# The second product of blocks 4 and 5 by Strassen's scheme, and prepared weights stored whole

## The chip, the cores and the metric

One core of a Trainium2 chip runs the whole program. The metric is device microseconds from start to end of one execution, as the median of several. On the core, PE (TensorE) multiplies matrices, DVE (VectorE) and ACT (ScalarE) do elementwise work, POOL (GpSimd) does a little at the start, and SP (SyncE) only issues DMAs. Each engine works its instructions in the order in which the program lists them.

## The reference

A windowed attention over 4 x 768 tokens gives x of 3072 x 512. Two dense layers follow, each with two products and a bend between them:

```
x   = attention(q, k, v, mem_k, mem_v)        # 3072 x 512
h   = x @ w_in1;   g = h * clip(h + 3, 0, 6) / 6;   x2  = g @ w_out1     # 512 x 2048, 2048 x 512
h2  = x2 @ w_in2;  g2 = max(0.01 * h2, h2);         out = g2 @ w_out2
```

All inputs but the weights are fp32; the weights come as 64-bit floats and are decoded on the chip.

## The kernel before, in words

**Tiling.** The 3072 tokens are six blocks of 512 columns (N), numbered 0 to 5. The 2048 hidden features are 16 tiles (f) of 128 rows, the 512 model features four tiles of 128. Every product is of fp32 values in two parts: a value is rounded to fp32r by a cast on ACT (high part), and DVE subtracts that from the value (low part). A product of two such values is three matmuls: high x high, low x high, high x low. So a plain tile of a product, 128 hidden rows against 512 model features and 512 tokens, is 4 x 3 = 12 matmuls of 128 x 128 by 512 columns (`hidden`, line 856, and `output`, line 903).

**Layer one, blocks 0 to 3,** is plain: `hidden` and `output` alternate, while the attention of later tokens runs between them. Blocks 0 and 1 run their first eight hidden tiles (partly in two half-width pieces for block 1), store a half sum of the output in DRAM (`half`), and add it when the other eight tiles are done.

**Pairs.** Blocks 4 and 5 are pair -1 of layer one; blocks 0-1, 2-3 and 4-5 are pairs 0, 1 and 2 of layer two. A pair's two blocks and the weights are cut into a 2 x 2 scheme, and a product of 2 x 2 quarters is made with seven quarter products instead of eight (Winograd's form of Strassen's scheme, numbers 1, 6, 5, 7 and then 2, 3, 4). `seven` (line 1136) makes the first product of a pair: for each of eight tiles i, seven products of 2 x 3 = 6 matmuls (line 1156), added up by DVE from four PSUM banks, then bent by ACT. Its banks are the set h, h, hx, hx for even i and the set of four y for odd i, but for pair -1 always h, h, hx, hx. `second` (line 1245) makes the second product of pairs 0 to 2: seven numbers n, and for each of them eight tiles i of 6 matmuls (line 1300); for each, ACT and DVE cut the right operand into high and low (lines 1288, 1289). `x_pair` (line 959) loads the right operands of a pair's first product from DRAM, forms the sums and cuts them: eight loads, 22 DVE and 14 ACT operations a pair. The second product of blocks 4 and 5 is plain: `output` for block 4 stands between the tiles of pair -1's first product, and block 5's bent values go to DRAM (`later`) and come back (`back_b`) for 16 tiles of `output` after it.

**Prepared weights.** `prepare` (line 1041) makes the seven left operands of tile i of weight 1i, 2i or 2o (first digit the layer; i the first product, o the second). For 2i and 2o it decodes two tiles (`decode`, line 354: one ACT and four DVE operations each, two of them with two tensor operands, into two `wm` buffers); for 1i it adds high and low again (`joined`). Then four sums of 256 columns are formed in place by DVE (line 1065) and all seven operands are cut into high and low parts of 256 columns (ACT line 305, DVE line 308) in `ys` buffers and stored to DRAM (`keep`, line 1032), 256 KB each. One preparation begins when the two `wm` buffers of the one before are done (`chain`). `left` (line 1087) loads two operands, both parts, 512 KB, into a `w` buffer when a product needs them; six such loads form a ring. There are 33 `w` buffers of 4 KB a partition for everything.

**What sets the order.** The program's text is written out by a planner (`schedule`, line 94). Each piece of work (`add`) has an engine, a duration, a key and the work it follows. A key counts PE work: 12 matmuls are 3 units. A piece is offered when its key is at most 60 units (`AHEAD`) ahead of progress; of the pieces offered the engine with the least key is taken first, where preparations count 60 units more (`late=LATE`). They also don't begin near the end of a plain output's sum (`ends`). The preparations' keys are the list `PLAN` plus `B0` = 24. Layer one's plain blocks are 68 items (pairs of `hidden` and `output`) of 6 units, so pair -1 begins at 408. `seq2` (line 328) is the order of PE's work from there on, and gives `pos_p` and `pos_q`, the positions of the products of `seven` and `second`. In `left` a load's key is 22 units before its product.

## Time and profile before

| | us |
|---|---|
| median of 3 runs | 1069.92 (1068.75 to 1071.33) |
| the profiled execution | 1069.66 |
| its span, first to last instruction | 1067.6 |
| PE busy | 1045.2 (7536 matmuls) |
| DVE busy | 777.5 |
| ACT busy | 569.0 |

The profile is of one execution. Busy shares are means over stages of different kinds: the start with attention, layer one up to 441 us, pair -1 with the plain outputs of blocks 4 and 5 up to 606.9 us, then six stages of 76.2 us: the first and the second product of pairs 0, 1 and 2. The chain of work that ended last tells what the end waited for; windows tell how full each engine is in each stage; timelines show when one instruction follows another. Recorded matmuls overlap, so their mean duration is not the time that one adds.

### The profile page before, as it was taken

The numbers are of one execution on the slowest core, as the hardware profiler recorded it, in microseconds if no ns is written. First come the engines' busy times: TensorE is split into PE (matmuls) and PEld (weight loads), VectorE is DVE, ScalarE is ACT, GpSimd is POOL, SyncE is SP. The second block draws the span as 40 slices with busy tenths as digits, with TensorE's granted clock in tenths as the row PEclk, the third lists the DMA queues.
The fourth block names the chain that finished last, engine by engine and source line by source line (L and its number), as shares of the span: only waits on it lengthen the run. The fifth ranks groups of instructions, "written<-read, shape, count | busy, mean of one in ns | idle before, by whom it ended". The sixth has DMA issues, their size and how long they took to land.

```text
span 1067.6 us, 20633 instructions
## 1 busy us (share of the span) xinstructions
PE 1045.2 (98%) x7536; PEld 864.4 (81%) x7536; DVE 777.5 (73%) x1469; ACT 569.0 (53%) x1416; POOL 14.5 (1%) x27
## 2 busy tenths in 40 slices
PE   5899999999999999999999999999999999999998
PEld 4778988888888888888888888888888888888886
DVE  4997993757776569898897688898465794465663
ACT  5678674656666666555456354565243553243432
POOL 2100000000000000000000000000000000000000
PEclk9899999999999999999999999999999999999999
DMA  9899234556776857899999599968656697666763
GB/s 208 221 245 279 104 112 132 184 164 191 222 223 198 260 180 251 285 313 323 321 332 355 199 344 358 341 213 321 229 208 233 243 321 248 217 232 227 269 214 119
DMA packets 124469, 257.22 MB, mean 241 GB/s; under 512 B 12752, under 2 KB 47056, under 8 KB 124368
## 3 DMA queue, kind: packets, MB, share of 16 engines
q1 hardware_dynamic: 124368, 255.90, 72.5%
q8 instruction: 60, 0.98, 0.4%
q14 instruction: 41, 0.34, 0.1%
HBM read 184.55 MB, written 71.30 MB: 240 GB/s over the span
## 4 chain that ended last, share of the span: by engine, by line
PE 91%; DMA 3%; DVE 2%; ACT 1%; SPq 1%; issue 1%; DVEq 0%; ACTq 0%
PE y L903 19%; PE h L856 15%; PE y L1300 12%; PE y L1156 11%; PE hx L1156 10%; PE h L1156 8%; PE h L1300 6%; PE hx L1300 3%; DMA w<-in_raw 2%; PE hx L903 2%; PE h L903 2%; PE at L533 2%; PE at L472 1%; PE at L522 1%; DMA w<-in_w1o 1%
## 5 line engine op out<-in xcount | busy, mean ns | idle before, releaser
L903 PE MATMUL y<-g,w 128*128 128x512 f32 (+1 forms) x1008 | 236.2, 382 | 0.1
L903 PEld LDWEIGHTS y<-g,w 128*128 128x128 f32 x1008 | 181.7, 188 | 36.1 <-ACT ys L933 0.3
L308 DVE TENSOR_TENSOR w<-w 128x512 fp32r<-128x512 f32 (+1 forms) x208 | 137.0, 688 | 17.6 <-ACT w L305 16.5
L856 PE MATMUL h<-xh,w 128*128 128x512 f32 (+1 forms) x544 | 131.6, 383 | 3.6 <-DVE xl L308 2.1
L856 PEld LDWEIGHTS h<-xh,w 128*128 128x128 f32 x544 | 98.4, 190 | 23.9 <-ACT xh L305 2.2
L1300 PE MATMUL y<-w 128*128 128x512 f32 x384 | 90.0, 389 | 0.0
L1131 ACT ACTIVATE w<-w 128x512 f32<-128x512 f32 x48 | 30.3, 632 | 107.8 <-DVE w L1214 79.2
L1300 PEld LDWEIGHTS y<-w 128*128 128x128 f32 x384 | 72.1, 188 | 15.0
L308 DVE TENSOR_TENSOR ys<-wm,ys 128x256 fp32r<-128x256 f32 x168 | 68.3, 426 | 19.3 <-ACT ys L305 18.5
L305 ACT CAST ys<-wm 128x256 fp32r<-128x256 f32 x168 | 62.7, 405 | 34.9 <-DVE wm L377 16.8
L1156 PE MATMUL hx<-w 128*128 128x512 f32 x336 | 80.7, 389 | 0.0
L868 ACT ACTIVATE r<-h,three 128x512 f32<-128x512 f32 (+1 forms) x68 | 45.4, 668 | 56.0 <-PE h L856 55.7
L1156 PEld LDWEIGHTS hx<-w 128*128 128x128 f32 x336 | 63.1, 188 | 13.1
L305 ACT CAST w<-w 128x512 fp32r<-128x512 f32 x116 | 66.8, 618 | 10.6 <-DVE w L308 3.8
L871 DVE SCALAR_TENSOR_TENSOR r<-r,h 128x512 f32<-128x512 f32 (+1 forms) x68 | 44.3, 652 | 36.5 <-ACT r L868 36.1
L856 PE MATMUL h<-xl,w 128*128 128x512 f32 (+1 forms) x272 | 70.8, 382 | 0.0
L305 ACT CAST g<-r 128x512 fp32r<-128x512 f32 (+1 forms) x86 | 52.0, 604 | 34.5 <-DVE r L871 21.5
L308 DVE TENSOR_TENSOR g<-r,g 128x512 fp32r<-128x512 f32 (+1 forms) x86 | 56.9, 662 | 15.8 <-ACT g L305 15.4
L305 ACT CAST g<-w 128x512 fp32r<-128x512 f32 x50 | 31.0, 623 | 59.3 <-PE y L1300 31.2
L856 PEld LDWEIGHTS h<-xl,w 128*128 128x128 f32 x272 | 49.5, 190 | 9.5
L308 DVE TENSOR_TENSOR g<-w,g 128x512 fp32r<-128x512 f32 x50 | 33.9, 689 | 26.9 <-ACT g L305 26.7
L1156 PE MATMUL y<-w 128*128 128x512 f32 x216 | 50.9, 389 | 0.0
(216 smaller groups left out, 1758.2 us busy)
## 6 DMA issues: line engine op xcount, KB each, us to landing
w<-kept2i SPq DMA_DIRECT2D x84, 512.0 KB
w<-kept2o SPq DMA_DIRECT2D x84, 512.0 KB
kept1i<-ys SPq DMA_DIRECT2D x56, 256.0 KB
kept2i<-ys SPq DMA_DIRECT2D x56, 256.0 KB
kept2o<-ys SPq DMA_DIRECT2D x56, 256.0 KB
w<-kept1i SPq DMA_DIRECT2D x28, 512.0 KB
w<-later SPq DMA_DIRECT2D x20, 512.0 KB
a<-in_raw SPq DMA_DIRECT2D x40, 224.0 KB
```

The lines of the kernel that those rows point to most:

```text
L305: nc.scalar.copy(out, in_) if e == "ACT" else engine(e).tensor_copy(out=out, in_=in_)
L308: engine(e).tensor_tensor(out=out, in0=a, in1=b, op=ALU.subtract)
L472: nc.tensor.matmul(ps.t[h * CHUNK:(h + 1) * CHUNK, par, i * W:(i + 1) * W], qk[h // 2].t[r, gp, (h % 2) * G + c * CHUNK:(h % 2) * G + (c + ...
L522: nc.tensor.transpose(pt.t[:, i // NC, (i % NC) * 128:(i % NC + 1) * 128], e.t[:, i].rearrange("p r k -> p (r k)"), ident)
L533: nc.tensor.matmul(pv.t[(h % 2) * D:(h % 2 + 1) * D, par, (h // 2) * 2 * G + i * CHUNK:(h // 2) * 2 * G + (i + 1) * CHUNK], v[h // 2].t[r, ...
L856: nc.tensor.matmul(h.t[:, :n], w.t[:, 1 if p == 1 else 0, k * 128:(k + 1) * 128], x[:, k, c0:c0 + n], start=(p == 0 and k == 0), stop=(p = ...
L868: nc.scalar.activation(out=make(r)[:, :n], in_=h.t[:, :n], func=AF.Relu, bias=three[:, 0:1], scale=1.0)
L871: nc.vector.scalar_tensor_tensor(out=r.t[:, :n], in0=r.t[:, :n], scalar=6.0, in1=h.t[:, :n], op0=ALU.min, op1=ALU.mult)
L903: nc.tensor.matmul(bank(banks[d])[:, c0:c0 + n], w.t[:, 1 if p == 1 else 0, d * 128:(d + 1) * 128], g.t[:, 1 if p == 2 else 0, :n], start= ...
L1131: return add(lambda e: nc.scalar.activation(out=at(), in_=at(), func=AF.Prelu, alpha=0.01), {"ACT": act(N)}, key, after=[after], uses=uses)
L1156: nc.tensor.matmul(bank(to), t.t[:, o, l, kt * 128:(kt + 1) * 128].bitcast(F32R), operand(p, name, 1 if q == 2 else 0, kt).bitcast(F32R), ...
L1300: nc.tensor.matmul(bank(to[d]), w.t[:, o, 1 if q == 1 else 0, d * 128:(d + 1) * 128].bitcast(F32R), g.t[:, 1 if q == 2 else 0], start=(fre ...
```

## The change

The second product of pair -1 is made by `second` too: the plain `output` calls of blocks 4 and 5, `back_b` and the extra `later` space are gone, and `seven` bends pair -1's sums with layer one's gate (`gated`, `bent`: a Relu on ACT and one operation on DVE, the second half of the buffer of sums as scratch) and keeps them as it does for the other pairs. `second`'s ends scale by 1/6 for pair -1 and store to `spill`. This needs prepared 1o weights: eight more calls of `prepare`.

1o, 2i and 2o are stored whole (`whole`): no cutting into high and low, the four sums are formed in two `ys` buffers, and each of the seven operands is stored as 128 KB. `left` loads four operands, 512 KB, into a `w` buffer, at most about seven half-loads ahead, and cuts two of them at a time into another `w` buffer with an ACT cast and a DVE subtraction of 512 columns (keys 12 units before the product, at most four such pieces ahead). The product's second part waits for the low half. 1i stays as it was, with a ring of five.

`PLAN` is new: 1i and 1o alternate, two per 18 units from key 140 on, then the eight 2i and the eight 2o, one per 18 units from 274 on. 1o preparations, and every second one of the first six of 2i and 2o, use the two `st` buffers and a chain of their own (`chains`). All of them wait until the last plain weights are cut. Layer one runs block 1's second eight tiles ahead of block 0's, and block 1 keeps its sum in PSUM without the way over DRAM. `x_pair` of pairs 0 to 2 has keys 24 and 16 units ahead of the stage. All pairs use alternating sets of banks.

The diff, cut to its core (the lines left out put the 1/6, the gate and `spill` into `seven` and `second`, and pass both waits on the parts of a left operand):

```diff
@@ -44,11 +44,14 @@
 LEFT_OF = {1: "a11", 2: "a12", 3: "s4", 4: "a22", 5: "s1", 6: "s2", 7: "s3"}
 ORDER = FIRST + THEN
 RING, OPS = 6, 6
+RING_LESS = 28
+BOTH = 6
+SPLIT = ("1i",)
+LEAD, RING_V, SPLITS = 28, 7, 4
 LATE, BEFORE = 60, 7
 JOINED = 8
-PLAN = [(172 + 16.5 * (k + k // 2), "1i", k) for k in range(8)]
-PLAN += [(172 + 16.5 * (3 * k + 2), ("2i", "2o")[k % 2], k // 2) for k in range(4)]
-PLAN += [(172 + 16.5 * (12 + k), ("2i", "2o")[k % 2], 2 + k // 2) for k in range(12)]
+PLAN = [(140 + 18 * (k // 2), ("1i", "1o")[k % 2], k // 2) for k in range(16)]
+PLAN += [(274 + 18 * k, ("2i", "2o")[k // 8], k % 8) for k in range(16)]
...
-    items += [("1", j, f, 0, N) for j in range(TWICE) for f in range(KF // 2, KF)]
+    items += [("1", j, f, 0, N) for j in (1, 0) for f in range(KF // 2, KF)]
...
-    for i in range(KF // 2 + 1):
-        if i < KF // 2:
-            seq2 += [("p", -1, i, n) for n in FIRST]
-            if i == 0:
+    for p in range(-1, PAIRED):
+        for i in range(KF // 2):
+            seq2 += [("p", p, i, n) for n in FIRST]
+            if p < 0 and i == 0:
                 seq2.append(("y", PLAIN - 1, KF - 1))
-            seq2 += [("p", -1, i, n) for n in THEN]
-        if i:
-            seq2 += [("y", PLAIN, 2 * i - 2), ("y", PLAIN, 2 * i - 1)]
-    seq2 += [("y", PLAIN + 1, f) for f in range(KF)]
-    for p in range(PAIRED):
-        for i in range(KF // 2):
-            seq2 += [("p", p, i, n) for n in FIRST + THEN]
+            seq2 += [("p", p, i, n) for n in THEN]
...
-        halves = (KF // 2, KF) if j < TWICE else (KF,)
+        halves = (KF // 2, KF) if j == 0 else (KF,)
         begin = c0 == 0 and f in (0, *halves)
         end = f + 1 in halves
         if begin:
-            ybuf[lay, j] = banks_of(j > PLAIN)
+            ybuf[lay, j] = banks_of(False)
...
+        k = add(lambda e: nc.vector.tensor_tensor(out=make(m, ([128, 512], F32)), in0=w.t[:, 0].bitcast(F32), in1=w.t[:, 1].bitcast(F32), op=ALU.add), {"DVE": dve(512)}, key, after=[*wtask[which, f], *splits[-2:], *gate], allocs=[m], uses=[w], late=LATE)
...
+    def whole(which, i, raws, l, key):
+        at = {"a11": (0, 0), "a12": (0, 256), "a21": (1, 0), "a22": (1, 256)}
+        if which[1] == "o":
+            at["a12"], at["a21"] = at["a21"], at["a12"]
+        sums = [Buf("ys"), Buf("ys")]
+        at |= {"s1": (2, 0), "s3": (2, 256), "s2": (3, 0), "s4": (3, 256)}
+        homes, made_by = [*raws, *sums], {}
+        def part(name):
+            c, o = at[name]
+            return made(homes[c])[:, o:o + 256]
+        def form(name, x, y, op):
+            new = homes[at[name][0]]
+            made_by[name] = add(lambda e: nc.vector.tensor_tensor(out=part(name), in0=part(x), in1=part(y), op=op), {"DVE": dve(256)}, key, after=[*l, *(made_by[n] for n in (x, y, "s1") if n in made_by)], allocs=[new] if at[name][1] == 0 else [], uses=[b for b in homes if b.users and (b is not new or at[name][1])], late=LATE)
+        def keep_whole(name):
+            q = [LEFT_OF[m] for m in ORDER].index(name)
+            slot = 7 * i + q if which[1] == "i" else KF // 2 * q + i
+            kdone[which, slot] = add(lambda e: nc.sync.dma_start(out=kept[which][slot // 4, :, slot % 4], in_=part(name)), {"SP": dma(131072, 300.0)}, key + 2, after=[made_by[name]] if name in made_by else l, uses=[homes[at[name][0]]], late=LATE)
+        for name in ("a11", "a12", "a22"):
+            keep_whole(name)
+        for name, x, y, op in (("s1", "a21", "a22", ALU.add), ("s2", "s1", "a11", ALU.subtract), ("s3", "a11", "a21", ALU.subtract), ("s4", "a12", "s2", ALU.subtract)):
+            form(name, x, y, op)
+            keep_whole(name)
...
-            line, place = (chain, "wm") if i < JOINED else (alone, "st")
+            line, place = (chain, "wm") if which != "1o" else (alone, "st")
             parts = [joined(which, 2 * i + c, key, place, line) for c in range(2)]
         else:
-            line, parts = chain, []
+            turn_of = len(decoded) // 2 % 2 and len(decoded) < 2 * BOTH
+            line, parts = chains[turn_of], []
             for c in range(2):
-                parts.append(decode(src, 2 * i + c, key + 6 * c, after=splits[-2:] + decoded[-2:-1], gate=chain, late=LATE))
+                parts.append(decode(src, 2 * i + c, key + 6 * c, after=splits[-2:] + decoded[-2:-1], gate=line, place=("wm", "st")[turn_of], late=LATE))
...
+        if which not in SPLIT:
+            whole(which, i, raws, l, key)
+            return
...
-        m = 7 * KF // 2 * (p + 1) + (7 * KF // 4 if which == "o" and p >= 0 else 0) + slot // 2
-        if p < 0:
-            m += 7 * KF // 4
+        m = 7 * KF // 2 * (p + 1) + (7 * KF // 4 if which == "o" else 0) + slot // 2
         which = ("1" if p < 0 else "2") + which
+        if m not in ring and which not in SPLIT:
+            group = slot // 4
+            if (p, which, group) not in loaded:
+                r = Buf("w")
+
+                def fn(e):
+                    nc.sync.dma_start(out=make(r, ([128, 4, 256], F32)), in_=kept[which][group])
+
+                k = add(fn, {"SP": dma(524288, 360.0)}, key - LEAD, after=[*(kdone[which, s] for s in range(4 * group, 4 * group + 4)), *rlast.get(m - RING_V, [])], allocs=[r])
+                loaded[p, which, group] = r, k
+            r, k = loaded[p, which, group]
+            t, o = Buf("w"), 2 * (slot // 2 % 2)
+            hi = add(lambda e: copy(e, make(t, ([128, 2, 2, 256], F32R))[:, :, 0], r.t[:, o:o + 2]), {"ACT": act(512)}, key - 12, after=[k, *rlast.get(m - SPLITS, [])], allocs=[t], uses=[r])
+            lo = add(lambda e: minus(e, t.t[:, :, 1], r.t[:, o:o + 2], t.t[:, :, 0].bitcast(F32)), {"DVE": dve(512)}, key - 11.5, after=[hi], uses=[r, t])
+            ring[m] = t, (hi, lo)
...
-            k = add(fn, {"SP": dma(524288, 360.0)}, key - 22, after=[kdone[which, slot], kdone[which, slot + 1], *rlast.get(m - RING + (p < 0), [])] + (xtask[-1, "b11" if slot < 4 else "t4"][slot >= 4][:1] if p < 0 else []), allocs=[t])
-            ring[m] = t, k
+            k = add(fn, {"SP": dma(524288, 360.0)}, key - 22, after=[kdone[which, slot], kdone[which, slot + 1], *rlast.get(m - RING + (m < RING_LESS), [])] + (xtask[-1, "b11" if slot < 4 else "t4"][slot >= 4][:1] if which == "1i" else []), allocs=[t])
+            ring[m] = t, (k, k)
...
-        product(part(0), N, [wl, *xhi, *need], allocs=alloc, uses=[u for u in us if u not in alloc], count=2)
-        product(part(1), N, [], uses=us, count=2)
+        product(part(0), N, [wl[0], *xhi, *need], allocs=alloc, uses=[u for u in us if u not in alloc], count=2)
+        product(part(1), N, [wl[1]], uses=us, count=2)
...
+        def bent(at, k, uses):
+
+            if p >= 0:
+                return leak(at, key, k, uses)
+            done["spare"] = [gated(at, at, [k, *done.get("spare", [])], u(1), [ut, *uses])]
+            return done["spare"][0]
...
+            k = product(part(order[:2]), N, [wl[0], hi, *need], allocs=to if fresh else (), uses=us + ([] if fresh else to), count=2)
+            product(part(order[2:4]), N, [wl[1]], uses=us + to, count=2)
...
-                x_pair(j + 1, pos_p[j + 1, 0, 1] - 58, 20)
+                x_pair(j + 1, pos_p[j + 1, 0, 1] - 24, 8)
             second(j, f, n[0])
         else:
-            if j > PLAIN:
-                if f == 0:
-                    x_pair(0, pos_p[0, 0, 1] - 40, 18)
-                back_b(f)
             output("1", j, f, 0, N)
```

## Rows read from the trace of the kernel before

**Rows 1.** The page: span and instructions; PE's busy tenths in 40 slices.
```profile
span 1067.6 us, 20633 instructions
...
PE   5899999999999999999999999999999999999998
```

**Rows 2.** Chain of work that ended last: start us, length us, what.
```profile
441.00 2.72 PE h L1156 x12
...
552.52 10.88 PE y L903 x48
606.92 2.72 PE h L1156 x12
...
683.08 10.88 PE h L1300 x48
...
759.24 2.72 PE h L1156 x12
...
1042.12 21.77 PE y L1300 x96
```

**Rows 3.** Windows by stage: us, busy (count) of PE PEld DVE ACT POOL, clock, DMA, GB/s.
```profile
36.40:120.00 83.60, 80.39 (x959) 68.14 (x960) 73.52 (x161) 62.44 (x189) 1.47 (x1) 0.97 0.80 228
120.00:441.00 321.00, 321.00 (x3239) 264.26 (x3238) 227.84 (x461) 197.77 (x607) 2.91 (x3) 1.00 0.61 191
441.00:606.90 165.90, 165.90 (x734) 137.37 (x733) 140.23 (x277) 85.60 (x166) 0.00 (x0) 1.00 0.88 309
606.90:683.10 76.20, 76.20 (x338) 63.10 (x337) 59.01 (x114) 36.75 (x74) 0.00 (x0) 1.00 0.97 341
683.10:759.20 76.10, 76.10 (x337) 63.00 (x337) 63.98 (x106) 40.72 (x72) 0.00 (x0) 1.00 0.75 272
759.20:835.40 76.20, 76.20 (x338) 63.10 (x337) 44.01 (x67) 27.55 (x45) 0.00 (x0) 1.00 0.66 233
835.40:911.60 76.20, 76.20 (x338) 63.10 (x337) 57.99 (x94) 38.37 (x70) 0.00 (x0) 1.00 0.76 264
987.70:1063.90 76.20, 76.18 (x337) 62.74 (x335) 45.35 (x72) 30.61 (x56) 0.00 (x0) 1.00 0.60 204
```

**Rows 4.** Timelines of DVE and ACT, layer two: start us, length us, engine, what.
```profile
730.81 5.50 DVE L308 TENSOR_TENSOR w<-w 128x512 f32<-128x512 f32 x9
...
700.86 0.62 ACT L305 CAST g<-st 128x512 fp32r<-128x512 f32 x1 [1.29 <-PE hx L1300]
701.38 0.62 ACT L305 CAST xh<-w 128x512 fp32r<-128x512 f32 x1
...
640.88 0.42 DVE L1065 TENSOR_TENSOR wm<-wm 128x256 f32<-128x256 f32 x1
641.21 0.69 DVE L1214 TENSOR_TENSOR w<-y,w 128x512 f32<-128x512 f32 x1
```

**Rows 5.** What DVE waited for, 441 to 606.9 us: us in total, times, longest.
```profile
DVE w L308 <- PE hx L903: 2.9, 2, 2.7
DVE xh L308 <- ACT xh L305: 2.9, 2, 2.2
```

**Rows 6.** Windows of 20 us (columns as in rows 3).
```profile
540.00:560.00 20.00, 20.00 (x90) 16.57 (x89) 19.40 (x38) 11.37 (x22) 0.00 (x0) 1.00 0.89 320
700.00:720.00 20.00, 20.00 (x90) 16.57 (x89) 20.00 (x35) 12.63 (x23) 0.00 (x0) 1.00 0.62 214
```

**Rows 7.** Single lines: decodes after 441 us, stores of prepared weights, and SP's waits.
```profile
L373 DVE SCALAR_TENSOR_TENSOR wm<-w,wm x22: 681/686/694, 442.6 to 657.6; 128x512 uint32<-128x512 uint32 x22
...
L1032 SPq DMA_DIRECT2D kept2o<-ys x56: 319/320/543, 299.2 to 673.3; - x56
...
SPq L1098 <- PE y L1300: 20.1, 15, 3.7
```

**Rows 8.** DMA issues of the page: operation, count, KB each.
```profile
w<-kept2i SPq DMA_DIRECT2D x84, 512.0 KB
w<-kept2o SPq DMA_DIRECT2D x84, 512.0 KB
kept1i<-ys SPq DMA_DIRECT2D x56, 256.0 KB
kept2i<-ys SPq DMA_DIRECT2D x56, 256.0 KB
kept2o<-ys SPq DMA_DIRECT2D x56, 256.0 KB
```

More of the change, by code (lines that the diff above doesn't have):

```diff
@@ L1028, in tile_attn_moe_moe2 @@
     chain, kdone, decoded, alone = [], {}, [], []
+    chains = (chain, alone)
     def keep(which, slot, src, after, uses, key):
@@ L1037, in joined @@
         w, m = wbuf[which, f], Buf(place)
-        k = add(lambda e: nc.vector.tensor_tensor(out=make(m, ([128, 512], F32)), in0=w.t[:, 0].bitcast(F32), in1=w.t[:, 1].bitcast(F32), op=ALU.add), {"DVE": dve(512)}, key, after=[*wtask[which, f], *gate], allocs=[m], uses=[w], late=LATE)
+        k = add(lambda e: nc.vector.tensor_tensor(out=make(m, ([128, 512], F32)), in0=w.t[:, 0].bitcast(F32), in1=w.t[:, 1].bitcast(F32), op=ALU.add), {"DVE": dve(512)}, key, after=[*wtask[which, f], *splits[-2:], *gate], allocs=[m], uses=[w], late=LATE)
@@ L1170, in put @@
         def put(r, after):
-            held["b", p, i] = add(lambda e: nc.sync.dma_start(out=later[p, i], in_=r.t), {"SP": dma(N * 512, 330.0)}, key, after=[after], uses=[r])
+            held["b", p, i] = add(lambda e: nc.sync.dma_start(out=later[p % (PAIRED + 1), i], in_=r.t), {"SP": dma(N * 512, 330.0)}, key, after=[after], uses=[r])
         def u(c):
@@ L1349, in second @@
                 before = [qdone[p, 5, d]] if n == 7 else [qdone[p, 6, d]]
-                q = plus(lambda s=s: s.t, from_, at(with_), key, [k, *before], allocs=[s], uses=[with_, bk])
+                q = sum_of(lambda s=s: made(s), at(with_), [k, *before], allocs=[s], uses=[with_, bk])
                 qdone[p, n, d] = q
```

102 lines of the change are left out of this document (40 added, 62 removed).

## The prediction

> **What bounds the kernel now.** I read three views, in this order. The page first: PE, the matrix engine, is busy in every slice of the span from the third on [rows 1]. A busy share alone proves little, since matmuls overlap in the record, so I read the chain of work that ended last for their spacing. It is nothing but PE work from 441 us to the end: 12 matmuls take 2.72 us, 48 take 10.88 us, 96 take 21.77 us [rows 2], so one costs 0.2267 us wherever it stands. A first-product stage of a layer-two pair is 8 x 7 x 6 = 336 matmuls = 76.2 us, and so is a second-product stage: the stages begin at 606.92, 683.08 and 759.24 us [rows 2]. Then the windows by stage: from 120 us on PE is busy for all of each window, at a granted clock of 1.00 [rows 3]. Nothing that DVE, ACT or the DMAs do after 120 us is waited for. The time is a count of matmuls, until another engine fills up. In these stages DVE is the nearest: 64.0 of 76.1 us in the second stage of pair 0, against 40.7 for ACT [rows 3].
>
> **Matmuls.** The plain second product of blocks 4 and 5 goes: 2 blocks x 16 tiles x 12 = 384. In its place come 8 tiles x 7 products x 6 = 336. The difference, 48 x 0.2267 = 10.88 us, lies wholly on the path.
> The Trainium skill, "TensorE: Matmul & The Clock Gate", section "Wait — 56ns, not 53.3ns?", gives 215.7 ns from start to start for 512 columns at full clock; the rows show 226.7 ns. By the page the 48 would be worth 10.4 us, as an estimate; the row is this kernel's own.
>
> **Splitting the left operands at each use.** The weights of 2i, 2o and 1o now come whole, so each stage that uses them gets 28 ACT casts and 28 DVE subtractions of 512 columns. Nine such DVE operations in a row take 5.50 us with 0.69 for one alone, so their pitch is (5.50 - 0.69)/8 = 0.60 us; ACT's casts start 0.52 us apart [rows 4]. That is 28 x 0.60 = 16.9 us of DVE and 28 x 0.52 = 14.6 us of ACT per stage. What it lies beside: the first stage of pair 1 has 67 DVE operations, its second stage 94 (22 of them from `x_pair`), the second stage of pair 2 has 72 [rows 3]. With 28 more, at 0.60 us: 57, 73.4 and 60 us of 76.2. It fits, by a thin 3 us where `x_pair` falls into the stage. ACT goes from 38.4 to 53 us in the same stage: covered. If DVE's cover is gone, each lacking operation costs PE 0.60 us.
>
> **Preparing the weights.** A 2i or 2o preparation loses seven halvings into high and low: 19 DVE operations become 12. Two-operand ones of 512 columns cost 0.60 us, those of 256 columns 0.33 [rows 4]; I take 0.33 for the two one-operand steps of a decode as well. So 4 x 0.60 + 8 x 0.33 = 5.1 us instead of 7.4. The eight new 1o preparations cost 2 x 0.60 + 4 x 0.33 = 2.5 us each, 20 us in all, before 441 us. Between 120 and 441 us DVE is busy 227.8 of 321.0 us [rows 3], so 93 us are free for them.
>
> **The stretch where DVE gets tight.** Today the first product of blocks 4 and 5 is mixed with the plain products, and 441 to 606.9 us has 140.2 us of DVE work in 165.9 [rows 3]. After the change three stages stand there: the first product of pair -1 (348 matmuls with the last tile of block 3, 78.9 us), its second product (76.2 us), and the first product of pair 0, up to some 7 us before its end, when the last 2o weights must be in DRAM to be read back and split (69 us). Together 224 us. DVE work in them without preparations, at 0.60 us: 102 operations (11 for each of 8 tiles, less 2 that fall later, and 16 run ahead for the second product) = 61.4 us; 122 (as counted for pair 1) = 73.4 us; about 75 = 45 us. Sum 180 us. The 44 us that remain hold 8.7 preparations of 5.1 us.
> How many are left at 441 us? In the trace 22 decodes run after 441 us, the last at 657.6 us [rows 7]: 11 of 16 preparations. In the new plan a 2i or 2o preparation has key 24 + 274 + 18k; progress at 441 us is 68 x 6 = 408. Work on key leaves 9; work as early as `AHEAD` = 60 allows leaves 6. The old plan ran all preparations through one chain of two `wm` buffers; the new one has two chains for 1i and 1o and for the first six of 2i and 2o, and DVE is freer there. I take 8: 180 + 41 = 221 of 224 us. The bounds are 211 us (6 left) and 226 us (9 left, 2 us too many).
> Can DVE be that full without PE waiting? From 700 to 720 us it was busy 20.00 of 20.00 us while PE lost nothing, and 19.40 from 540 to 560 [rows 6]. So the likeliest cost is small. I take 1.4 us, three preparations' last operations arriving late by some 0.5 us; bounds 0 and 9 us (9 left at a DVE filled to 97%: 226/0.97 - 224). Below nothing is excluded, since PE has no idle here to give back.
>
> **Edits costed at nothing, with their cover.** `x_pair` of pairs 0 to 2: its eight loads pass SP's queue, its 22 DVE and 14 ACT operations get later keys (24 instead of 58 or 40 units before the stage, a unit being 0.907 us). All are needed within 10 us of the next stage's start. Hidden by DVE's spare 3 us and by PE's run-ahead of some 8 units in both operands; without that, up to 22 x 0.60 = 13 us for each pair, at least 0. DMA: 168 loads of 512 KB become 84, and 14 are added; stores shrink from 256 to 128 KB [rows 8]. The 0.97 share of the first stage of pair 0 [rows 3] falls. New waits: ACT's cast waits for the load's landing, with the casts of the right operands and the activations queued behind it; a load waits on SP for four stores, with spills, output stores and later loads behind it; the second part of each product waits for the low half. Today loads of left operands stand on SP for a free buffer up to 3.7 us [rows 7] and PE does not notice, because they are issued 22 units ahead; the new ones have 28. Layer one's new order saves four evictions on ACT and eight DMAs; PE has no idle there, so nothing is gained, and the 3.2 us idle of 36.4 to 120 us [rows 3] bounds what could move. PSUM: pair -1 takes the two alternating sets of banks that pairs 0 to 2 use without a wait [rows 3].
>
> **Sum.** The profiled execution took 1069.66 us, 0.26 under the median of 1069.92. 1069.66 - 10.88 + 1.4 = 1060.2 us.
>
> **The rivals.**
> (A) Forecast: DVE holds. 1058.8 to 1061.8 us. For it: 20.00 of 20.00 us without a wait [rows 6]. Against it: 221 of 224.
> (B) DVE runs somewhat short: 8 or 9 preparations left and DVE filled to 97%. 221/0.97 - 224 = 4 us, 226/0.97 - 224 = 9 us: 1062.5 to 1067.5 us. For it: no plan so far had to hold 97% over 200 us.
> (C) Slower: DVE is in order and idles while work waits behind an operation whose ACT cast or load is not done. In 441 to 606.9 us it reached 84.5% (140.2 of 165.9) though preparations were waiting for their turn [rows 3]. At 90%: 221/0.90 - 224 = 21.6 us lost at the second products of pairs -1 and 0, 1080 us. It beats the gain from a share of 221/(224 + 10.9) = 94% downwards. Against it: the idle is made of single waits for PE or ACT, the longest two of 2.9 us each in sum [rows 5], which a longer list of ready work can fill, and the last 2o store was done 9.8 us before its stage (673.3 against 683.08) [rows 7, 2].
> The Trainium skill, "TensorE: Matmul & The Clock Gate", Part 1 on the HAM clock gate, says that a PE left idle drops to half clock, which would deepen (C); no window after 120 us shows less than 1.00.
> (D) Buffers: 33 `w` buffers must now hold raw loads and split pieces. A border between stages loses up to 3.7 us [rows 7], at two of the seven borders 7 us: 1066 us, up to 1069 us with a third.
>
> **How the numbers follow.** A 0.62, B 0.20, C 0.10, D 0.08. The range leaves out C, the upper part of D, and little else: below it reaches 0.8 us under the sum without any loss, for the scatter of the runs (1068.75 to 1071.33), above to the end of B: 1058.0 to 1067.5 us. A measurement of this kernel can tell about 0.2%, 2.1 us, from no change. Faster by more: A, B and half of D, 0.85. Slower: C, 0.10. Within: 0.05.
>
> **What would show it.** Matmuls 7536 - 48 = 7488, still 2.72 us for twelve. The first stage of pair 1 at about 57 us of DVE, its second at about 73. Pair 0's stages begin about 596 and 672 us, plus what was lost. If A holds, PE is busy in every window from 120 us on, bar a few tenths. If B or C holds, PE idles released by DVE, before the second products of pairs -1 and 0, and pairs 1 and 2 show none. If D, the idle stands at the first product after a border, released by a DMA or an ACT cast. What would make the prediction wrong most cheaply is the count of preparations left at the start of pair -1: above ten the gain is gone.

## The result and the profile after

The changed kernel takes 1075.34 us (median; 1074.47 to 1077.26) against 1069.61 us for the kernel before on the same chip (1068.62 to 1071.33). The ratio is 1.0052, with a 95% interval of 1.0039 to 1.0064: slower by half a per cent, where the forecast was 1060.2 us. The profiled execution of the changed kernel took 1077.26 us with a span of 1075.5 us; it is the slowest of its runs, 1.9 us over the median, and the accounts below are made against it and against the 1069.66 us of the profiled execution before.

The page of the changed kernel: span, busy time by engine, PE and DVE in 40 slices.
```profile
span 1075.5 us, 20609 instructions
...
PE 1041.2 (97%) x7488; PEld 858.9 (80%) x7488; DVE 906.9 (84%) x1661; ACT 640.7 (60%) x1515; POOL 20.3 (2%) x30
...
PE   5899999998999999999999899999999999999998
...
DVE  4997997767776668889999999999888899687895
```
The 48 matmuls are gone (7488 are left). But PE has two slices of 8 where [rows 1] had none after the second slice, one before 270 us and one about 600 us, and DVE is at 9 in ten slices in a row.

The windows by stage (columns as in rows 3). The first two are parts of layer one, then come the first and the second product of the new pair -1, the two of pair 0, the two of pair 1 and the second of pair 2.
```profile
200.00:260.00 60.00, 56.70 (x696) 46.50 (x695) 43.06 (x86) 30.16 (x105) 1.56 (x1) 0.97 0.80 234
...
380.00:451.30 71.30, 68.94 (x570) 56.65 (x569) 58.04 (x111) 37.17 (x86) 1.47 (x1) 0.98 0.79 246
451.30:530.00 78.70, 78.70 (x349) 64.98 (x348) 71.50 (x131) 34.03 (x55) 0.00 (x0) 1.00 0.90 309
530.00:614.30 84.30, 79.38 (x337) 63.75 (x337) 84.20 (x142) 57.91 (x106) 0.00 (x0) 0.98 0.49 165
614.30:690.50 76.20, 76.20 (x338) 63.02 (x337) 75.01 (x138) 43.27 (x78) 0.00 (x0) 1.00 0.73 228
690.50:766.70 76.20, 76.20 (x337) 62.91 (x336) 76.20 (x128) 53.80 (x99) 0.00 (x0) 1.00 0.53 175
766.70:842.90 76.20, 76.20 (x338) 63.12 (x337) 59.61 (x95) 40.19 (x71) 0.00 (x0) 1.00 0.40 138
842.90:919.10 76.20, 76.20 (x338) 63.12 (x337) 73.47 (x122) 53.62 (x99) 0.00 (x0) 1.00 0.49 166
995.30:1071.50 76.20, 76.20 (x337) 62.89 (x335) 59.66 (x97) 44.15 (x81) 0.00 (x0) 1.00 0.36 121
```
Read the second and the fourth number of each row. From pair 0 on PE is busy all the time, as in [rows 3]. Before that, PE is not busy all the time in two places: in layer one, and in the second product of pair -1 (530.00 to 614.30), which should take 76.2 us and takes 84.3, while DVE is busy for 84.20 of them.

The chain of work, start of the first products of pairs -1 and 0 (start us, length us, what):
```profile
451.28 2.72 PE h L1184 x12
...
614.46 2.72 PE h L1184 x12
```
[Rows 2] has 441.00 and 606.92 at the same two points. So layer one takes 451.28 - 441.00 = 10.28 us more. What lay between the two points took 165.92 us, should take 165.92 - 10.88 = 155.04, and takes 614.46 - 451.28 = 163.18: 8.14 us lost. 10.28 - 10.88 + 8.14 = 7.54 us, of the 7.60 us by which the two profiled executions differ. The rest of the kernel is the same.

PE's timeline in these two places, the pieces that stood behind an idle time or beside one (start us, length us, what, idle before it and what ended that):
```profile
251.48 0.87 PE L517 MATMUL at<-ident,a 128*128 128x128 f32 x6 [1.08 <-POOL a L513]
254.57 2.68 PE L528 MATMUL at<-a 64*64 64x32 f32 x96 [2.22 <-ACT a L308]
257.18 3.73 PE L898 MATMUL y<-g,w 128*128 128x512 f32 x12
...
393.60 0.80 PE L467 MATMUL at<-a 64*32 64x64 f32 x57 [2.35 <-issue]
...
531.75 2.11 PE L1318 MATMUL h<-g,w 128*128 128x512 f32 x8 [0.58 <-DVE g L311]
...
609.40 0.73 PE L1318 MATMUL y<-w 128*128 128x512 f32 x2 [4.35 <-DVE w L311]
609.97 4.50 PE L1318 MATMUL y<-g,w 128*128 128x512 f32 x12
```
The longer wait costs a second time. After the 4.35 us at 605 us the twelve matmuls from 609.97 on take 4.33 us to the next start (614.30, where pair 0 begins in this view), and 2.72 otherwise; the granted clock of that stretch is shown further down.

### The profile page after: what moved, and what is told of

Its sections match the earlier page's. It is cut to its first block, busy times and chain, and to the rows that moved or that the text cites. A ratio compares the mean times of both kernels' runs of the same rounds, so it can differ in the third digit from the quotient of the medians.

```text
span 1075.5 us, 20609 instructions
## 1 busy us (share of the span) xinstructions
PE 1041.2 (97%) x7488; PEld 858.9 (80%) x7488; DVE 906.9 (84%) x1661; ACT 640.7 (60%) x1515; POOL 20.3 (2%) x30
## 4 chain that ended last, share of the span: by engine, by line
PE 78%; DVE 11%; DMA 5%; ACT 2%; issue 2%; SPq 1%; DVEq 0%; ACTq 0%
PE h L851 15%; PE y L898 14%; PE y L1318 13%; PE y L1184 12%; PE hx L1184 7%; PE h L1318 6%; PE h L1184 5%; DVE w L311 5%; PE hx L1318 3%; PE at L528 2%; DMA kept1o<-ys 1%; DMA w<-in_raw 1%; PE at L467 1%; DVE g L311 1%; ACT a L497 1%
## 5 line engine op out<-in xcount | busy, mean ns | idle before, releaser
L311 DVE TENSOR_TENSOR w<-w 128x512 fp32r<-128x512 f32 (+1 forms) x446 | 291.1, 688 | 21.2 <-ACT w L308 20.9
L898 PE MATMUL y<-g,w 128*128 128x512 f32 (+1 forms) x816 | 192.6, 383 | 0.1
L308 ACT CAST w<-w 128x512 fp32r<-128x512 f32 x330 | 187.5, 617 | 5.7 <-DVE w L311 2.7
L898 PEld LDWEIGHTS y<-g,w 128*128 128x128 f32 x816 | 147.7, 190 | 29.3 <-ACT ys L928 0.3
L1318 PE MATMUL y<-w 128*128 128x512 f32 x504 | 118.5, 389 | 4.3 <-DVE w L311 4.3
L1318 PEld LDWEIGHTS y<-w 128*128 128x128 f32 x504 | 94.5, 188 | 24.5 <-DVE w L311 5.0
L1184 PE MATMUL y<-w 128*128 128x512 f32 x336 | 78.8, 389 | 0.0
L308 ACT CAST g<-w 128x512 fp32r<-128x512 f32 x68 | 42.2, 623 | 57.1 <-PE y L1318 34.3
L1184 PEld LDWEIGHTS y<-w 128*128 128x128 f32 x336 | 63.0, 188 | 13.2
L1318 PE MATMUL y<-g,w 128*128 128x512 f32 x264 | 65.2, 397 | 0.0
L1318 PEld LDWEIGHTS y<-g,w 128*128 128x128 f32 x264 | 50.6, 192 | 11.0 <-DVE g L311 0.3
L1318 PE MATMUL h<-w 128*128 128x512 f32 x252 | 59.2, 389 | 0.0
L1184 PE MATMUL hx<-w 128*128 128x512 f32 x240 | 57.6, 389 | 0.0
```

The costliest lines, as they stand in the source:

```text
L308: nc.scalar.copy(out, in_) if e == "ACT" else engine(e).tensor_copy(out=out, in_=in_)
L311: engine(e).tensor_tensor(out=out, in0=a, in1=b, op=ALU.subtract)
L898: nc.tensor.matmul(bank(banks[d])[:, c0:c0 + n], w.t[:, 1 if p == 1 else 0, d * 128:(d + 1) * 128], g.t[:, 1 if p == 2 else 0, :n], start= ...
L1184: nc.tensor.matmul(bank(to), t.t[:, o, l, kt * 128:(kt + 1) * 128].bitcast(F32R), operand(p, name, 1 if q == 2 else 0, kt).bitcast(F32R), ...
L1318: nc.tensor.matmul(bank(to[d]), w.t[:, o, 1 if q == 1 else 0, d * 128:(d + 1) * 128].bitcast(F32R), g.t[:, 1 if q == 2 else 0], start=(fre ...
```

## The experiments

Two explanations were on the table. Capacity (called S, or A, in the expectations): the second product of pair -1 asks more operations of DVE than 76.2 us hold, wherever they stand. Buffers (Y): in layer one the eight new 1o preparations hold the `ys` buffers that layer one's own sums need. The rivals were the order of DVE's work (the right operands of pair 0 come too late), the late preparations (T), and relief by the idle engine POOL. One table first, for all the runs that follow; "begins" is the first matmul of a first product in PE's timeline, "ops" are DVE's operations in pair -1's second product. Each ratio is to the kernel before as timed on the same chip as the run (1068.98 to 1069.70 us).

| kernel | time us (range) | ratio to before (95%) | pair -1 begins | pair 0 begins | between | ops |
|---|---|---|---|---|---|---|
| before | 1069.61 (1068.62 to 1071.33) | 1 | 440.84 | 606.76 | 165.92 | - |
| changed | 1075.34 (1074.47 to 1077.26) | 1.0052 (1.0039 to 1.0064) | 451.11 | 614.30 | 163.19 | 142 |
| e1_pool_low | 1089.7 (1088.3 to 1090.58) | 1.0190 (1.0174 to 1.0205) | 447.91 | 618.11 | 170.20 | - |
| e2_xpair_early | 1076.1 (1073.22 to 1078.24) | 1.0062 (1.0041 to 1.0083) | 447.86 | 610.08 | 162.22 | 141 |
| e3_1o_ys2 | 1077.66 (1075.26 to 1078.15) | 1.0073 (1.0054 to 1.0091) | 441.67 | 614.43 | 172.76 | 163 |
| e4_pool_all | 1099.44 (1099.04 to 1100.56) | 1.0284 (1.0268 to 1.0299) | 446.55 | 614.43 | 167.88 | - |
| e5_low_half | 1068.87 (1066.46 to 1069.31) | 0.9988 (0.9978 to 0.9998) | 447.86 | 603.62 | 155.76 | 132 |
| e6_low_all_ys2 | 1063.18 (1062.91 to 1064.22) | 0.9940 (0.9924 to 0.9956) | 444.85 | 599.89 | 155.04 | 133 |
| e8_prep_less | 1076.95 (1075.35 to 1078.0) | 1.0066 (1.0047 to 1.0084) | 449.50 | 613.78 | 164.28 | 138 |
| e9_ready | 1065.98 (1062.68 to 1066.62) | 0.9964 (0.9951 to 0.9977) | 445.11 | 601.89 | 156.78 | 133 |
| e10_ready_plan | 1061.17 (1059.83 to 1061.96) | 0.9919 (0.9905 to 0.9934) | 442.75 | 598.82 | 156.07 | 130 |
| e12_plan_alone | 1070.7 (1068.31 to 1072.1) | 1.0005 (0.9995 to 1.0015) | 441.09 | 604.97 | 163.88 | 146 |

(e7_whole_alone and e11_whole_keys are built on the kernel before; they stand at the end.)

### Relief by another engine: e1_pool_low and e4_pool_all

```diff
-  lo = add(... minus(...), {"DVE": dve(512)}, key - 11.5, ...)
+  lo = add(... minus(...), {"DVE": dve(512), "POOL": pool(512)}, key - 11.5, ...)
```


> Only change against the kernel after: the low half of a split left operand may run on POOL as well as on DVE. Theory A (in the second product of pair -1 DVE has more work than time; the loss there is its capacity): with POOL's help the 4.35 us wait at 609 us falls below 1.5 us, pair -1 takes 155 to 158 us from the first matmul of its first product to the first of pair 0, instead of 163.2, and the time is 1067 to 1070 us. The idle near 250 us in layer one stays. Rival B (the order: x_pair's block of 11 operations stands ahead of the last low halves on DVE): the block stays ahead, the wait stays above 3 us, 1074 to 1076 us. Rival P (POOL and DVE hinder each other): DVE's operations start more than 0.64 us apart where POOL runs, and less than half of the 8 us comes back.

e4_pool_all has this too, and gives POOL six of the 512-wide differences of each `x_pair` (`sub`) and the four 256-wide sums of each whole preparation.

> Low halves of left operands on DVE or POOL, the four sums of a whole preparation on POOL, x_pair's second to fourth difference on POOL. If A and Y hold (layer one's read-back comes clear of the 1o stores as the preparations' order moves), no PE idle above 1 us after 120 us: 1059 to 1063 us, 0.7 to 1.0% under the kernel before. If rival P holds, DVE's pitch grows and the time stays above 1068 us. If layer one's idle comes from the order of the blocks, 3.3 us and a slower clock after it stay: 1065 to 1068 us.

Both are slower, by 1.9 and 2.8%. PE's longest wait in e1_pool_low from 440 to 640 us (total us, times, longest), and POOL's group there:
```profile
PE hx L1318 <- POOL w L311: 6.1, 1, 6.1
...
L311 POOL TENSOR_TENSOR w<-w 128x512 fp32r<-128x512 f32 x10 | 37.3, 3753 | 198.3 <-DVE w L1210 147.3 <-ACT w L308 51.0
```
A low half takes 3753 ns on POOL in the mean, five times the 0.69 us that DVE takes, and PE waits for one of them longer than it waited for anything after 120 us in the changed kernel. Nor does DVE run as before. Its low halves of the right operands, from 530 to 600 us in e1_pool_low and from 530 to 614.3 in the changed kernel:
```profile
L311 DVE TENSOR_TENSOR g<-w,g 128x512 fp32r<-128x512 f32 x12 | 10.2, 867 | 0.4 <-ACT g L308 0.4
```
```profile
L311 DVE TENSOR_TENSOR g<-w,g 128x512 fp32r<-128x512 f32 x18 | 12.3, 691 | 0.0
```
867 ns against 691, because two of the twelve took 3.50 us together (from 581.96 us, while POOL was at work). It also goes the other way: one of POOL's subtractions lasts 11.31 us (from 540.88 us, the one behind the wait of 6.1 us), while DVE runs two-operand operations without a pause at its usual pace, 0.60 us from start to start. What POOL takes beside an idle DVE no run shows. So POOL is no place for this work. e4_pool_all loses in every pair: after pair 0 has begun PE waits another 13.6 us in it, 7.1 of them for POOL. The Trainium skill, "GPSIMD Engine Reference", section "1. Specifications", lists POOL's SBUF interface as shared with VectorE, in contention with DVE instructions that have two SBUF inputs. These rows agree with that.

### The order on DVE: e2_xpair_early

```diff
-                x_pair(j + 1, pos_p[j + 1, 0, 1] - 24, 8)
+                x_pair(j + 1, pos_p[j + 1, 0, 1] - 40, 18)
```


> Only change: x_pair of pairs 0 to 2 has keys 40 and 22 units ahead of its stage again instead of 24 and 16. Theory A (capacity): the waits move to an earlier place in the second product of pair -1, their sum stays at 5 us within 1.5, pair -1 still takes 161 to 166 us, time 1073 to 1078 us. Rival B (order): with x_pair out of the way of the last low halves the wait is gone, pair -1 takes 155 to 157 us, time 1067 to 1069 us.

The right operands of pair 0 come earlier and the wait at 605 us goes; in its place stand others, from 440 to 640 us:
```profile
PE y L1318 <- DVE g L311: 3.1, 1, 3.1
PE h L1318 <- DVE g L311: 1.4, 2, 0.9
PE h L1318 <- DVE w L311: 0.4, 1, 0.4
```
4.9 us, as in the changed kernel (0.58 + 4.35), and the two stages take 162.22 us instead of 163.19. The loss moves and stays, so it does not come from this order.

### The buffers of layer one: e3_1o_ys2

```diff
-        sums = [Buf("ys"), Buf("ys")]
+        sums = [Buf("ys", 2 if which == "1o" else 99) for _ in range(2)]
```
The two buffers for the sums of a 1o preparation may only be taken if no more than two of the four `ys`, the one taken included, are then in use.

> Only change: a 1o preparation takes its two ys buffers only when no other ys buffer is in use, so that it can't hold them while the half sum of block 0 is read back. Theory Y (layer one's loss near 250 us: the read-back waits for ys buffers whose 1o stores have not landed, and DVE, in order, waits behind it): no PE idle between 240 and 260 us, pair -1 begins 4 to 7 us earlier than at 451.3 us. Rival L (the new order of blocks 0 and 1 alone): the 3.3 us idle stays. The 1o preparations end later, so the preparations of 2i and 2o do too, and by theory A pair -1 then loses more, 10 to 18 us: total 1074 to 1084 us.

The changed kernel shows this ahead of the stall at 250 us: ACT's first copies into the buffers in which layer one collects its output wait for stores of prepared 1o weights, three times, 4.5 us in all.
```profile
ACT ys L934 <- DMA kept1o<-ys: 4.5, 3, 2.3
...
244.68 0.19 ACT L934 COPY ys<-three 128x1 f32<-128x1 f32 x1 [0.32 <-DMA kept1o<-ys]
```
From there the chain of work leads to PE (start us, length us, what):
```profile
241.35 3.22 DMA kept1o<-ys
...
244.68 0.06 ACT ys L934
...
244.78 1.88 ACT a L497 x12
...
249.44 3.14 DMA ys<-half
252.57 0.61 DVE r L866
...
254.57 2.68 PE at L528 x95
```
A store of a 1o sum lands, ACT can make its copy and goes on to the attention's exponentials behind it; the load of the first half of layer one's sums comes late, DVE's `r` behind that, ACT's copy behind that, and PE last.
In e3_1o_ys2 the same window is clean, here beside that of the changed kernel above (200 to 260 us):
```profile
200.00:260.00 60.00, 60.00 (x720) 1.00 0.67 208
```
(PE alone: busy, clock, DMA share, GB/s.) Pair -1 begins at 441.67 us, 0.83 us after the kernel before and not 10.27. So the buffers are the cause of layer one's loss. One part of that loss stays apart, the 2.35 us at 391 us, for which the trace of the changed kernel names no one ("issue"); it was 0.59 and 1.14 us in e1_pool_low and e2_xpair_early, which have the same layer one, and pair -1 begins 3.2 us earlier in these. The buffers are not the whole gain, though: the preparations, held back, now fall into pair -1's second product, 163 operations in 93.9 us, and PE waits 5.2 and 5.5 us there. What layer one got back was lost again.

### Capacity: e5_low_half, e8_prep_less, e6_low_all_ys2

```diff
+            if which == "1o" and slot // 2 % 2:
+                lo = add(lambda e: copy(e, t.t[:, :, 1], r.t[:, o:o + 2]), {"ACT": act(512)}, key - 11.5, ...)
+            else:
                 lo = add(lambda e: minus(e, t.t[:, :, 1], ...), {"DVE": dve(512)}, key - 11.5, ...)
```


> Every second of the 28 low halves of the left operands of the new second product (pair -1) is made by an ACT copy of the sum; its subtraction on DVE is left out, so the output differs. That takes 14 DVE operations of 0.60 us, 8.4 us, out of pair -1 and puts 14 of 0.52 us on ACT. Theory S (the second stage of pair -1 asks more of DVE than its 76.2 us hold, about 138 operations of 0.60 us = 83 us, whatever the preparations do): the 8.1 us lost in pair -1 shrink to about 1, pair -1 takes 155 to 157 us and the kernel 1067 to 1069.5 us, the stall at 250 us staying. Rival T (late preparations fill whatever DVE leaves, so the freed time goes to them): pair -1 stays above 160 us and the kernel above 1072.5.

With 14 of the 28 subtractions left out the two stages take 155.76 us, where 155.04 is what the matmuls alone ask for. The row of pair -1's second product:
```profile
526.70:603.60 76.90, 76.60 (x337) 63.10 (x337) 76.90 (x132) 63.93 (x119) 0.00 (x0) 1.00 0.58 188
```
DVE is busy for all of the 76.90 us and PE loses 0.3. DVE filled to the brim costs next to nothing; with ten operations more the stage takes 84.30 us.

The counter-test takes DVE work out of the preparations instead:
```diff
-        k2 = add(low, {"DVE": dve(512)}, key + 0.4, after=[k], ...)
+        k2 = k if own else add(low, {"DVE": dve(512)}, key + 0.4, after=[k], ...)
```


> The changed kernel with the last DVE operation of each layer-two decode left out (the one that puts in the three lowest bits of the mantissa, 512 columns): 32 operations less in all, 16 of them after pair -1 has begun, 9.6 us of DVE. Theory S (pair -1's second stage asks too much of DVE by itself; few preparations fall into it): 1073 to 1076 us and pair -1 still 161 us or more. Rival T (the preparations outstanding at its start are what fills DVE): pair -1 157 us or less and the kernel 1066 to 1069 us.

PE's wait in it, and its row of the same stage:
```profile
PE y L1318 <- DVE w L311: 4.3, 1, 4.3
...
528.60:613.80 85.20, 80.25 (x337) 64.42 (x338) 83.05 (x138) 56.86 (x104) 0.00 (x0) 0.96 0.50 165
```
32 operations less in all, and the wait is the same 4.3 us. No operation of a preparation lies in this window, and 138 operations, 83.05 us of DVE, still stand in it. So the work without preparations is 138 operations of 83.05/138 = 0.602 us, and the preparations (rival T) are not what overfills the stage.

e6_low_all_ys2 joins both remedies: the condition of e5_low_half without `slot // 2 % 2` (all 28), and the edit of e3_1o_ys2.

> All 28 low halves of pair -1's left operands for the second product are ACT copies (28 subtractions, 16.9 us of DVE, left out; the output differs), and the whole sums of the 1o weights hold at most two of the four ys buffers. Theory S+Y (the two stalls, DVE in pair -1 and ys buffers in layer one, are all that stands between the counted gain and the result): both go, pair -1 begins near 441 us and takes 155 to 156.5 us, and the kernel takes 1058 to 1061 us, what the prediction had. Rival (a third cost, such as later preparations in pairs 0 and 1 or the clock): 1064 or more, with the loss after 600 us.

The two stages take 155.04 us, to the hundredth what the matmuls ask for. The time of 1063.18 us is 2.2 us over the upper end of what was expected, and it is all in layer one: pair -1 begins at 444.85 us instead of 441.67, after waits of PE for casts and a load in the attention units (1.6 and 0.8 us). Why these stand in this run and not in e3_1o_ys2 was not settled. After 600 us PE waits 0.2 us, so the rival of a third cost there falls.

### A kernel that has both remedies and leaves nothing out: e9_ready, e10_ready_plan, e12_plan_alone

Layer one multiplies by the 1o weights in parts, so three of the seven forms, the ones that are no sums, lie in SBUF split already. They can be stored from there in parts: 12 of the 28 left operands then need no cast and no subtraction at use.
```diff
+READY = {0: "a11", 4: "a12", 6: "a22"}
...
         for name in ("a11", "a12", "a22"):
-            keep_whole(name)
+            if which == "1o":
+                c, o = at[name]
+                w, slot = wbuf["1o", 2 * i + c], KF // 2 * [LEFT_OF[m] for m in ORDER].index(name) + i
+                kdone[which, slot] = add(... nc.sync.dma_start(out=kept["1o", 2][slot // 2, :, slot % 2], in_=w.t[:, :, o:o + 256].bitcast(F32)) ...)
+            else:
+                keep_whole(name)
...
-        if m not in ring and which not in SPLIT:
+        ready = which == "1o" and slot // (KF // 2) in READY
+        if m not in ring and which not in SPLIT and not ready:
```


> The changed kernel, with nothing left out: three of the seven forms of the 1o weights (a11, a12, a22, no sums) lie in SBUF as hi and low halves already, since layer one uses them so; they are stored from there in parts, and 12 of pair -1's 28 left operands of the second product are loaded parted. That takes 12 DVE subtractions (12 x 0.60 = 7.2 us) and 12 ACT copies out of pair -1's second stage and holds the ys buffers for the four sums alone. Theory S (q-1 asks too much of DVE by itself): pair -1 takes 155 to 157.5 us instead of 163; with layer one's stall as it was, 1067 to 1070 us, and less if that stall shrinks too. Rival: the 24 larger stores (+3 MB) and 12 loads of 0.5 MB in place of 6 (+3 MB) delay others, and pair -1 stays above 160 us: 1073 or more.

Pair -1's two stages take 156.78 us, as capacity has it, and the time is 1065.98 us, below the range that was given for an unchanged layer one: the stall at 250 us is gone, and a smaller one (1.03 + 0.93 + 0.60 us) stands at 354 to 359. Why it moved was not followed up; the due times of the next run clear it.

```diff
-PLAN = [(140 + 18 * (k // 2), ("1i", "1o")[k % 2], k // 2) for k in range(16)]
-PLAN += [(274 + 18 * k, ("2i", "2o")[k // 8], k % 8) for k in range(16)]
+PLAN = [(140 + 18 * k, "1i", k) for k in range(8)] + [(150 + 14 * k, "1o", k) for k in range(8)]
+PLAN += [(250 + 14 * k, "2i", k) for k in range(8)] + [(422 + 18 * k, "2o", k) for k in range(8)]
```


> The kernel of the run before this one, and the preparations spread differently: 1i at 140 + 18k, 1o at 150 + 14k instead of both at 140 + 18 (k // 2), 2i at 250 + 14k, 2o at 422 + 18k instead of all sixteen at 274 + 18k. Theory S+Y (DVE in pair -1's second stage and the ys buffers in layer one are the whole loss): no stall of 1 us or more after 120 us, pair -1 begins at 441 to 445 us and takes 155 to 156.5 us: 1058.5 to 1063 us, faster than both kernels. Rival (earlier preparations collide with layer one's own work): pair -1 begins after 449 us and the time is 1066 or more.

All of PE's waits in it from 120 us to the end, and its row of pair -1's second product:
```profile
PE at L469 <- issue: 0.2, 1, 0.2
PE h L1326 <- DVE g L313: 0.2, 1, 0.2
PE y L1192 <- DVE w L1160: 0.2, 1, 0.2
...
521.30:598.80 77.50, 77.15 (x339) 63.18 (x338) 77.50 (x130) 53.20 (x98) 0.00 (x0) 1.00 0.64 223
```
1061.17 us, 0.81% below the kernel before (ratio 0.9919, 0.9905 to 0.9934): 8.5 us on the same chip, of the 10.88 us of the 48 matmuls, are there once both places have room.

Are the new due times enough by themselves? e12_plan_alone has them without the ready parts.

> The changed kernel with the due times of the preparations as in the run with parted forms and new due times, and nothing else: the low halves stay 28 in pair -1. Theory S: the due times can clear layer one's stall (pair -1 begins at 441 to 446 us) but not pair -1, which takes 162 us or more: 1067 to 1072 us. Rival T (preparations in pair -1 are what fills DVE, and earlier ones relieve it): pair -1 157 us or less, 1060 to 1064 us.

Pair -1 begins at 441.09 us, as before the change, but its two stages take 163.88 us, and PE waits 5.5 us at 595 to 600. 1070.7 us is the time of the kernel before. The due times cure layer one and the ready parts cure pair -1, each alone.

### One part of the change alone: e7_whole_alone, e11_whole_keys

Built on the kernel before: 2i and 2o are kept whole and parted at use (`whole`, `left` and the order of waits taken over from the change), the second product of pair -1 stays plain. (The expectation's count of 7680 matmuls was a slip; it is 7536.)

> The kernel before with one part of the change alone: 2i and 2o are kept whole and parted when loaded; the second product of pair -1 and the order of layer one stay as before, no 1o is prepared, and 7680 matmuls run. Theory: this part costs DVE 28 operations in each stage of pairs 0 to 2 and takes 7 out of each of 16 preparations; where pair 0's second stage holds 73 to 76 us of DVE work in 76.2 it just fits, so 1068 to 1071 us, no change. Rival (parting at use is itself what costs): pair 0's second stage loses 3 us or more and the kernel takes above 1073.

1082.26 us (1080.35 to 1083.46), ratio 1.0115 (1.0095 to 1.0134): slower, not the same. e11_whole_keys adds the change's due times for the next pair's right operands.
```diff
-                x_pair(j + 1, pos_p[j + 1, 0, 1] - 58, 20)
+                x_pair(j + 1, pos_p[j + 1, 0, 1] - 24, 8)
```


> The run with whole storage of 2i and 2o alone, and with the change's due times for the right operands of pairs 1 and 2 (24 and 8 in place of 58 and 20). Theory O (in pair 0's second stage DVE is so near full that the 44 operations of the next pair's right operands delay the halves that PE waits for when they come early): the two stalls at 720 and 744 us (1.6 and 4.9) go, 1068 to 1075 us. Rival (demand alone, wherever these 44 stand, as in pair -1): the loss moves and stays, above 1078.

1076.5 us (1075.51 to 1078.04), ratio 1.0065 (1.0050 to 1.0080), between the two expectations. The rows of pair 0's two stages in e7_whole_alone (first two) and e11_whole_keys:
```profile
608.80:685.00 76.20, 76.20 (x338) 63.10 (x337) 52.14 (x81) 38.81 (x71) 0.00 (x0) 1.00 0.42 146
685.00:767.00 82.00, 75.49 (x323) 61.48 (x322) 80.04 (x133) 55.91 (x103) 0.00 (x0) 0.96 0.45 151
```
```profile
606.70:683.00 76.30, 76.30 (x338) 63.20 (x337) 52.18 (x81) 38.90 (x71) 0.00 (x0) 1.00 0.43 147
683.00:765.30 82.30, 78.44 (x340) 64.48 (x339) 80.84 (x135) 55.49 (x103) 0.00 (x0) 0.98 0.45 151
```
It is the same picture in another pair: DVE idles for 24 us in the first stage and overflows in the second, with 133 and 135 operations where the changed kernel has 128 there (690.50 to 766.70) and loses nothing. The due times took away PE's two long waits (1.6 and 4.9 us, at 720 and 740 us), and one of 3.9 us came at the end of the stage, where e7_whole_alone has none. Why the changed kernel lets some more of these operations run in the first stage was not tried.

## Why the prediction was wrong, step by step

**Right: the matmuls.** 7488 are left, twelve take 2.72 us, and the 10.88 us come off between the two points of the chain before anything is lost there.

**Right for the stages in the sum, lucky for one that was not: the splitting in pairs 0 to 2.** Predicted were 57, 73.4 and 60 us of DVE in the stages of pair 1 (both) and in the second of pair 2; the rows show 59.61, 73.47 and 59.66, and 53.62 of ACT where 53 stood. The thin spare of 3 us was enough. But the prediction left out the fullest stage, pair 0's second: 63.98 us and 106 operations [rows 3], so by its own figures 63.98 + 16.9 = 80.9 us against 76.1. In e7_whole_alone it comes out so, 133 operations and 80.04 us of DVE, and the stage takes 82.00 us. In the changed kernel 128 operations stand there, DVE is busy for 76.20 of 76.20 us and PE does not wait; that it just fitted was luck.

**Right: the count of preparations.** Eight of 16 were left when pair -1 began: the last operation of a decode, after 451 us.
```profile
L372 DVE SCALAR_TENSOR_TENSOR wm<-w,wm x16: 680/684/692, 468.0 to 671.7; 128x512 uint32<-128x512 uint32 x16
```
The prediction called this count the cheapest way to go wrong. The count was right, and the e8_prep_less run shows that it hardly mattered.

**Wrong: the tight stretch as one sum.** The step that failed is "102 operations (... and 16 run ahead for the second product) = 61.4 us; 122 (as counted for pair 1) = 73.4 us; about 75 = 45 us", set against 224 us in all. Of the 16 only three ran ahead. DVE's work in pair -1's first product, of which three lines: decodes (eight; a decode has four operations), low halves of left operands (three), and an operation of the gate with DVE's idle time before it. Then the loads of the left operands, from when on, and ACT's first casts of right operands:
```profile
L372 DVE SCALAR_TENSOR_TENSOR wm<-w,wm 128x512 uint32<-128x512 uint32 x8 | 5.5, 684 | 0.0
...
L311 DVE TENSOR_TENSOR w<-w 128x512 fp32r<-128x512 f32 x3 | 2.0, 682 | 0.0
...
L1210 DVE SCALAR_TENSOR_TENSOR w<-w,h 128x512 f32<-128x512 f32 x4 | 2.7, 682 | 2.6 <-ACT w L1209 2.6
...
L1127 SPq DMA_DIRECT2D w<-kept1o x14: 319/372/722, 514.8 to 586.8; - x14
...
529.33 1.13 ACT L308 CAST g<-w 128x512 fp32r<-128x512 f32 x2
```
Of the 131 operations in that stage 8 x 4 + 13 = 45 belong to preparations (13 are whole sums), so 86 are its own: 16 fewer than 102, since 13 of the 16 came later and some last operations of the tiles did too. The second product has 142, of which 4 belong to a preparation, so 138 are its own: 122 + 16. The code kept them back: the left operands are split at most four pieces ahead of their use (`SPLITS` = 4; their loads begin at 514.8 us, 15 us before the stage), and the first six casts of right operands come in the program only behind the last tile's bent sum (`c_of[p, KF // 2 - 1, "22"]` in `second`), at 529.33 us. So DVE idled for 78.70 - 71.50 = 7.2 us in the first stage, mostly behind PE and ACT, and was short in the next. Loosening these two limits was not tried. At 0.602 us each (e8_prep_less) 76.2 us hold some 127 operations; 138 are 83.1 us, 6.9 too many, and with the four of a preparation that is about the 84.20 us of the row. PE waits 4.93 us in two waits, and with slow matmuls and short delays of single matmuls it is 8.14. A total of 221 of 224 us says nothing when the work can't cross from one stage to the next.

**Wrong: an edit costed at nothing.** The prediction gave the 1o preparations room on DVE before 441 us ("93 us are free for them") and layer one's new order no cost, "PE has no idle there, so nothing is gained". The engine time was there; the `ys` buffers were not. This part of the prediction looks at queues, landing and PSUM, but not at who else uses the pool of buffers that a new step takes from. It costs 10.28 us in the profiled execution, some 7 in others (pair -1 begins at 447.86 us in e2_xpair_early and e5_low_half, where this part is the same).

**The sum again.** 1069.66 - 10.88 + 10.28 + 8.14 = 1077.20 us; measured 1077.26. The forecast had +1.4 for both losses. Pair -1's loss alone would have given 1066.9 us.

**The rivals.** (B) had the right engine and, with 4 to 9 us, the right size, but not the cause: it priced preparations that were left over, and e8_prep_less says that they are not it. Nor had it the place: the long wait stands near the end of pair -1's second product, and pair 0's second product has none. (C) fails in the main: where PE waits, DVE was busy 84.20 of 84.30 us. Its mechanism, DVE idle behind PE and ACT, shows in the stage before, where DVE idled 7.2 us. (D) fails: PE waits at no border for a DMA or a cast. No rival had layer one in it, which is why the time left the range; the share of DVE at which a loss begins, 94% in (C), says nothing about a single stage, since stages run at 100% with at most 0.4 us lost (e5_low_half, pair 0, e10_ready_plan) once their operations number some 130 or fewer.
The sentence on the clock under (C) did come true. After the waits the granted clock falls; two windows about them:
```profile
249.00:262.00 13.00, 9.70 (x127) 7.92 (x126) 11.08 (x21) 4.39 (x11) 1.56 (x1) 0.87 0.94 294
604.00:614.30 10.30, 5.95 (x19) 4.43 (x18) 10.20 (x19) 4.14 (x7) 0.00 (x0) 0.83 0.14 36
```
After waits of 2.22 and 4.35 us the means are 0.87 and 0.83, a mixture of the two levels of 2.4 and 1.2 GHz. The Trainium skill, "TensorE: Matmul & The Clock Gate", Part 1, says that an idle PE falls back to the lower level; the rows agree. Of the 8.14 us lost in pair -1, 4.93 are the two waits; the slow matmuls behind the longer one are 4.33 - 2.72 = 1.61 more, and delays of single matmuls, too short to be listed as waits, the rest.

## What to carry to other kernels

Set an engine's work against the room of each stage by itself, and let work cross a border only as far as the trace or the code (keys, pieces ahead, buffers) lets it; here 138 operations stood against 127 while the stage before had 7 us idle. Put every stage into the sum, the fullest first. A new step has to be charged to every pool it takes a buffer from, and what waits there is whoever comes next in order, even where all engines have time. And before moving work to an idle engine, look for data that lie in the wanted form already: storing three forms as layer one uses them took 12 operations out of the tight stage, and with new due times made the idea worth its 0.8%.

## What the runs showed of the hardware

POOL takes 3753 ns in the mean for a subtraction of 128x512 fp32 beside a full DVE, and 11.31 us for one beside an unbroken run of two-operand operations on DVE (e1_pool_low); at other moments it is DVE that is held up, two operations for 3.50 us. DVE holds 100% for a stage of 76 us without PE waiting (pair 0's second product). Its operations of 512 columns last 0.69 us in the record but follow each other at 0.602 us (138 in 83.05 us, e8_prep_less), so the spacing, not the length, says how many a stage holds. The wait of 2.35 us at 391 us, to which the trace gives no cause, was 0.59 and 1.14 us in e1_pool_low and e2_xpair_early, with the same layer one; what makes it longer or shorter stays open.
